# A cross-attention and MLP kernel: first MLP layer contracted over softmax slots, softmax with tokens on partitions, layers of different batches interleaved

## Chip, cores, metric

The kernel runs on one core of a Trainium2 chip. The metric is the device time of one execution in microseconds (us), lower is better. Each comparison uses executions of the kernel before on the same chip.

## The reference

Eight batches, eight heads, 512 tokens of 64 elements, and 32 state slots per head. Tokens attend to state slots, slots attend to tokens, the two results are stacked to 544 rows per batch with the heads side by side (512 wide), and an MLP with a leaky ReLU follows.

```python
B, H, S, Ns, D = (8, 8, 512, 32, 64)
scores = scale * x @ state.T                 # [B,H,512,32]
a = softmax(scores);  xread = a @ state      # token rows
a2 = softmax(scores.T over tokens); sread = a2 @ x   # state rows
x = concat([xread, sread], axis=2) -> [8*544, 512]
h = x @ w_in                                 # 512 -> 2048
g = maximum(0.01 * h, h)
out = g @ w_out                              # 2048 -> 512, float32
```

(Condensed; the reference subtracts the row maximum in each softmax, neither kernel does.)

## The kernel before

Attention is done for pairs of heads with the slots on partitions. Its result, `xbT`, is the MLP input, transposed. The MLP works on chunks of 512 rows, and its tiles are taken from a queue, one between any two attention pieces.

```python
# attention of a pair of heads (cut)
nc.tensor.matmul(sc[:], lhsT=BDT[:], rhs=xT[:])            # [64 slots, 512 tokens]
nc.scalar.activation(out=ET[:], in_=sc[:], func=Exp, scale=SCALE, accum_out=r2[:])
...  # r1c: sums over slots by matmul; pa: transpose of a2; psr: state rows
nc.tensor.matmul(xr[:], lhsT=st.BDbf[:], rhs=ET[:])        # unnormalised xread
...
nc.tensor.matmul(rr1b[:, t * P:(t + 1) * P], lhsT=bcl[:, t], rhs=ident[:])   # 1/sum, spread out
nc.vector.tensor_tensor(out=xbT[st.k][:, ...], in0=st.xr_sb[:], in1=rr1b[:], op=mult)

# first layer, one of 16 tiles of a chunk: K = 512, four matmuls (cut)
for kt in range(4):
    nc.tensor.matmul(ph[:, :n], lhsT=w_in_bf[kt][:, 128 * j:128 * (j + 1)],
                     rhs=xbT[kt][:, tok0:tok0 + n], start=(kt == 0), stop=(kt == 3))
nc.scalar.activation(out=t01[:, :n], in_=ph[:, :n], func=Identity, scale=0.01)
nc.vector.tensor_tensor(out=hT[:, j, :n], in0=ph[:, :n], in1=t01[:, :n], op=max)

# second layer, one of 4 tiles of a chunk
for j in range(16):
    nc.tensor.matmul(py[:], lhsT=hT[:, j, t * P:(t + 1) * P], rhs=w_out_bf[j][:], ...)
nc.scalar.copy(ysb[:], py[:]);  nc.sync.dma_start(out[r0:r0 + P, :], ysb[:])
```

The softmax here doesn't subtract the row's maximum and nothing guards it: scores larger than these inputs give would overflow.

## Time and profile before

| | before |
|---|---|
| median of the first runs | 348.24 us |
| span of the profiled run | 347.2 us |
| TensorE (PE) busy | 307.3 us, 88% |
| matmuls of the first layer | 512 of N=512, 64 of N=256 (as long as 544 of N=512) |
| matmuls of the second layer | 544 of N=512 |
| one middle batch | 35.25 us |

From the page of the kernel before: the line of busy times, the row of PE over 40 slices of the span (tenths of busy time, 9 is 90% or more), and the chain that ended last, by engine and by line (the view cuts this line short).

```profile
PE 307.3 (88%) x1821; PEld 142.0 (41%) x1856; DVE 188.9 (54%) x487; ACT 152.1 (44%) x371; POOL 29.5 (8%) x70
...
PE   0115678999999999999999999999999999999995
...
PE 84%; DMA 9%; issue 3%; DVE 2%; ACT 1%; ACTq 0%; DVEq 0%
PE ph L196 35%; PE py L217 33%; DMA w_out_stage<-in_moe_w_out_dram 4%; DMA w_in_stage<-in_moe_w_in_dram 4%; PE rr1b L175 3%; PE sc L106 3%; PE xr L137 2%; PE pa L143 2%; PE pxt L96 2%; PE r1c L129 2%; DMA stf<-in_state_dram 1%; PE psr L152 
```

From the eighth slice on PE is busy for 90% or more of nearly every slice, and it owns 84% of the chain. "Busy" counts the latency of pipelined matmuls, so the distance between starts is the better measure. From the timeline of PE (start, duration, what):

```profile
125.96 0.38 PE L196 MATMUL ph<-xbT_90,w_in_bf_94 128*128 128x512 bf16 x1
126.27 0.40 PE L106 MATMUL sc<-xT,BDT 128*64 128x512 bf16 x1
126.60 0.39 PE L196 MATMUL ph<-xbT_91,w_in_bf_95 128*128 128x512 bf16 x1
```

A 128x512 matmul is shown as 0.38 us long, but in an undisturbed row the next one starts 0.216 us later. Around the score matmul (the middle line), which uses 64 columns of the array, the starts are 0.31 and 0.33 us apart. Two lines of the chain in order of time, the same instruction in two successive batches, give the time of a batch:

```profile
180.05 0.34 PE rr1b L175 x4
...
215.30 0.34 PE rr1b L175 x4
```

Of its 35.25 us, 124 matmuls of 0.216 us are the MLP (26.8 us: 15 first-layer and 4 second-layer tiles, by the weight loads from 180.05 to 215.30), and 8.5 us are the attention, with small waits. A batch's share of the MLP is 136 matmuls; the loop takes only 19 tiles per batch from the queue, and the rest runs after the last attention. Busy time by stretch (length, then each engine, clock, DMA share, GB/s):

```profile
core 0: us, PE busy (x) PEld busy (x) DVE busy (x) ACT busy (x) POOL busy (x), PEclk, DMA share, GB/s
0.00:20.00 20.00, 1.33 (x6) 0.57 (x6) 6.89 (x16) 0.00 (x0) 6.42 (x14) 1.00 0.85 275
20.00:40.00 20.00, 10.00 (x61) 4.79 (x63) 11.06 (x36) 6.10 (x17) 1.85 (x5) 1.00 0.80 204
40.00:60.00 20.00, 15.59 (x96) 6.75 (x97) 13.47 (x39) 9.03 (x26) 2.60 (x6) 1.00 0.45 122
180.00:215.25 35.25, 34.62 (x214) 15.68 (x217) 20.39 (x56) 17.16 (x44) 3.24 (x8) 1.00 0.23 63
```

In the first 60 us PE is busy for 26.9; in the middle nearly always.

### The profile page before, as it was taken

The numbers are of one execution on the slowest core, as the hardware profiler recorded it, in microseconds if no ns is written. First come the engines' busy times: TensorE is split into PE (matmuls) and PEld (weight loads), VectorE is DVE, ScalarE is ACT, GpSimd is POOL, SyncE is SP. The second block draws the span as 40 slices with busy tenths as digits, with TensorE's granted clock in tenths as the row PEclk, the third lists the DMA queues.
The fourth block names the chain that finished last, engine by engine and source line by source line (L and its number), as shares of the span: only waits on it lengthen the run. The fifth ranks groups of instructions, "written<-read, shape, count | busy, mean of one in ns | idle before, by whom it ended". The sixth has DMA issues, their size and how long they took to land.

```text
span 347.2 us, 5237 instructions
## 1 busy us (share of the span) xinstructions
PE 307.3 (88%) x1821; PEld 142.0 (41%) x1856; DVE 188.9 (54%) x487; ACT 152.1 (44%) x371; POOL 29.5 (8%) x70
## 2 busy tenths in 40 slices
PE   0115678999999999999999999999999999999995
PEld 0012233444444444444444444444444444444472
DVE  0655468851795359724991289318951693084070
ACT  0032227632764256524653466326641662264171
POOL 0510111100100011000100010001000000000000
PEclk9999999999999999999999999999999999999999
DMA  7897563123222222213121312110001000100201
GB/s 274 250 261 208 131 188 74 32 67 93 65 61 55 74 64 49 47 64 91 41 58 64 93 33 61 35 69 23 1 33 60 32 0 30 71 21 16 77 31 60
DMA packets 44666, 26.55 MB, mean 76 GB/s; under 512 B 37728, under 2 KB 37728, under 8 KB 44128
## 3 DMA queue, kind: packets, MB, share of 16 engines
q1 hardware_dynamic: 41760, 17.84, 18.6%
q10 hardware_dynamic: 2880, 8.39, 7.2%
q8 instruction: 14, 0.23, 0.3%
q14 instruction: 12, 0.10, 0.1%
HBM read 17.30 MB, written 8.91 MB: 75 GB/s over the span
## 4 chain that ended last, share of the span: by engine, by line
PE 84%; DMA 9%; issue 3%; DVE 2%; ACT 1%; ACTq 0%; DVEq 0%
PE ph L196 35%; PE py L217 33%; DMA w_out_stage<-in_moe_w_out_dram 4%; DMA w_in_stage<-in_moe_w_in_dram 4%; PE rr1b L175 3%; PE sc L106 3%; PE xr L137 2%; PE pa L143 2%; PE pxt L96 2%; PE r1c L129 2%; DMA stf<-in_state_dram 1%; PE psr L152 1%; PE pbd L101 1%; ACTq L64 0%; ACT ET L110 0%
## 5 line engine op out<-in xcount | busy, mean ns | idle before, releaser
L217 PEld LDWEIGHTS <-hT 128*128 128x128 bf16 x544 | 50.4, 98 | 59.6 <-issue 3.7
L224 ACT COPY ysb<-py 128x512 f32<-128x512 f32 x34 | 19.9, 585 | 86.7 <-PE py L217 60.4
L196 PE MATMUL ph<-xbT_90,w_in_bf_94 128*128 128x512 bf16 (+1 forms) x141 | 52.2, 372 | 1.0 <-DVE xbT_90 L181 0.8
L196 PE MATMUL ph<-xbT_89,w_in_bf_93 128*128 128x512 bf16 (+1 forms) x140 | 52.0, 374 | 1.0 <-DVE xbT_89 L181 0.4
L196 PE MATMUL ph<-xbT_91,w_in_bf_95 128*128 128x512 bf16 (+1 forms) x139 | 51.5, 373 | 0.3 <-DVE xbT_91 L181 0.2
L196 PE MATMUL ph<-xbT_88,w_in_bf_92 128*128 128x512 bf16 (+1 forms) x135 | 50.0, 374 | 0.4 <-issue 0.3
L110 ACT ACTIVATE ET<-sc 64x512 bf16<-64x512 f32 x32 | 18.9, 589 | 23.2 <-PE sc L106 20.1
L92 POOL CAST X2b<-X2f 128x512 bf16<-128x512 f32 x32 | 21.3, 664 | 75.6 <-PE psr L152 64.0
L98 DVE COPY xT<-pxt 128x512 bf16<-128x512 bf16 x32 | 13.3, 417 | 22.0 <-PE pxt L96 21.9
L196 PEld LDWEIGHTS <-w_in_bf_95 128*128 128x128 bf16 x144 | 14.1, 98 | 17.5 <-issue 6.7
L86 POOL MEMSET BDbf<- 64x128 bf16 x32 | 7.7, 244 | 143.5 <-PE xr L137 126.0
L196 PEld LDWEIGHTS <-w_in_bf_94 128*128 128x128 bf16 x144 | 14.2, 99 | 13.6
L129 PE MATMUL r1c<-hi,ET 64*128 64x2 bf16 x128 | 8.0, 164 | 13.2 <-ACT ET L110 12.8
L139 ACT CAST xr_sb<-xr 128x512 bf16<-128x512 f32 x32 | 18.9, 590 | 1.5 <-PE xr L137 0.3
L87 DVE CAST BDbf<-stf 32x64 bf16<-32x64 f32 x32 | 6.1, 191 | 24.3 <-POOL BDbf L86 15.4
L101 PE MATMUL pbd<-ident,BDbf 64*128 64x64 bf16 x32 | 6.4, 201 | 13.0 <-DVE BDbf L88 10.7
L196 PEld LDWEIGHTS <-w_in_bf_92 128*128 128x128 bf16 x144 | 14.2, 99 | 8.0 <-issue 1.8
L196 PEld LDWEIGHTS <-w_in_bf_93 128*128 128x128 bf16 x144 | 14.1, 99 | 8.1 <-issue 1.0
L129 PEld LDWEIGHTS <-ET 64*128 64x128 bf16 x128 | 5.3, 95 | 28.6 <-ACT ET L110 25.7
L106 PE MATMUL sc<-xT,BDT 128*64 128x512 bf16 x32 | 13.8, 430 | 3.2 <-DVE xT L98 2.4
L165 DVE CAST bcl<-rr1c 128x512 bf16<-128x512 f32 x32 | 14.2, 444 | 0.8
L96 PE MATMUL pxt<-ident,X2b 128*128 128x128 bf16 x128 | 13.7, 233 | 0.0
(489 smaller groups left out, 568.1 us busy)
## 6 DMA issues: line engine op xcount, KB each, us to landing
out_dram<-ysb SPq DMA_DIRECT2D x34, 256.0 KB, 2.0
X2f<-in_x_dram SPq DMA_DIRECT2D x64, 128.0 KB, 2.7
w_in_stage<-in_moe_w_in_dram ACTq DMA_DIRECT2D x4, 1024.0 KB, 6.2
w_out_stage<-in_moe_w_out_dram ACTq DMA_DIRECT2D x16, 256.0 KB, 3.2
stf<-in_state_dram SPq DMA_DIRECT2D x64, 8.0 KB, 1.9
```

Of the source, the lines that this page charges most:

```text
L92: nc.gpsimd.tensor_copy(X2b[:], X2f[:])
L96: nc.tensor.transpose(pxt[:, t * P:(t + 1) * P], X2b[:, t, :], ident[:])
L98: nc.vector.tensor_copy(xT[:], pxt[:])
L106: nc.tensor.matmul(sc[:], lhsT=BDT[:], rhs=xT[:], start=True, stop=True)
L110: nc.scalar.activation(out=ET[:], in_=sc[:], func=mybir.ActivationFunctionType.Exp, scale=SCALE, accum_out=r2[:],)
L129: nc.tensor.matmul(r1c[:, 2 * t:2 * t + 2], lhsT=ET[:, t * P:(t + 1) * P], rhs=hi[:], start=True, stop=True,)
L139: nc.scalar.copy(xr_sb[:], xr[:])
L165: nc.vector.tensor_copy(bcl[:], rr1c[:, :].rearrange("p (t h) -> p t h", h=2)[:, :, :, None].to_broadcast([P, 4, 2, D]),)
L175: nc.tensor.matmul(rr1b[:, t * P:(t + 1) * P], lhsT=bcl[:, t, :, :].rearrange("p h d -> p (h d)"), rhs=ident[:], start=True, stop=True,)
L196: nc.tensor.matmul(ph[:, :n], lhsT=w_in_bf[kt][:, 128 * j:128 * (j + 1)], rhs=xbT[kt][:, tok0:tok0 + n], start=(kt == 0), stop=(kt == 3),)
L217: nc.tensor.matmul(py[:], lhsT=hT[:, j, t * P:(t + 1) * P], rhs=w_out_bf[j][:], start=(j == 0), stop=(j == 15),)
L224: nc.scalar.copy(ysb[:], py[:])
```

## The change

Because the token rows are `a @ state`, the first layer is `a @ (state @ w_in)`. The change computes M = state @ w_in per batch (256 slots x 2048) and contracts the normalised softmax `a` with it: K is 256 instead of 512, so two matmuls per tile. `a` is computed with tokens on partitions and transposed once. The state rows of all batches are gathered and go through the MLP together. The leaky ReLU is one ACT instruction. First-layer tiles of batch b+2 and attention of b+3 stand between second-layer quarters of b. Inputs are loaded in larger pieces.

```diff
+    def m_chunk(b, n):                     # M = state @ w_in, 64x32 array tiles
+        pm = psum.tile([P, 2, 512], FP32, name="pm", tag="big")
+        for k in range(NK):
+            for g in range(2):
+                sl = slice(64 * g, 64 * (g + 1))
+                nc.tensor.matmul(pm[32 * k:32 * (k + 1), g, :], lhsT=bd[sl, b, k, g, :],
+                                 rhs=w_in_bf[n][sl, k, :], start=True, stop=True)
+        nc.vector.tensor_copy(st.M[n][:], pm[:])
 ...
-                for kt in range(4):
-                    nc.tensor.matmul(ph[:, :n], lhsT=w_in_bf[kt][...], rhs=xbT[kt][...], ...)
-                nc.scalar.activation(out=t01, in_=ph, func=Identity, scale=0.01)
-                nc.vector.tensor_tensor(out=hT, in0=ph, in1=t01, op=max)
+        for g in range(2):
+            nc.tensor.matmul(ph[:], lhsT=st.M[n][:, g, P * jj:P * (jj + 1)], rhs=st.aT[:, g, :],
+                             start=(g == 0), stop=(g == 1))
+        nc.scalar.activation(out=st.hT[:, j, :], in_=ph[:], func=Prelu, alpha=0.01)
 ...
+    load_state(); load_x(0); load_w_in(0); load_x(1); load_w_in(1); load_x(2) ...   # casts on DVE
+    for b in range(AHEAD):                 # AHEAD = 2
+        cast_x(b); att_xT(b, 0); att_xT(b, 1); att_scores(b); att_sread(b); att_aT(b)
+    ...                                    # M and first layer of batches 0 and 1
+    for b in range(B):
+        for t in range(4):
+            for q in range(4):
+                ffn2(b, t, q)
+                if b + AHEAD < B:
+                    ffn1(b + AHEAD, 4 * t + q)
+                for f in pieces.get(4 * t + q, []):      # attention and M of batch b + 3
+                    f()
```

The order that the tile scheduler builds differs somewhat from this order at the start.

## The prediction

> **What bounds the kernel now.** TensorE. The page has PE busy 88% of a 347.2 us span, granted clock full in every slice, and the chain of waits is 84% PE (first layer 35%, second 33%). The timeline shows N=512 matmuls starting 216 ns apart. Each layer has 544 (the profile's weight loads of the second), so 1088 x 216 ns = 235 us. The rest is the attention's small matmuls and a bad start: by the stretches table PE is busy only 27 of the first 60 us while DMA moves about 200 GB/s in 256-byte packets. One middle batch takes 35.25 us (rr1b at 180.05, 215.30).
>
> **Removed.** Token rows: first layer contracts over K=256 (2 matmuls per tile instead of 4). 8x16x2=256 matmuls, 55.3 us, plus state rows 64 of N=256 (about 109 ns, half of 216), 7.0 us, against 117.5 us. xr, rr1b, pbd, pa, r1c and their evictions go. The leaky ReLU becomes one ACT instruction (585-590 ns, as the 128x512 evictions now take) instead of ACT and a 692 ns DVE max.
>
> **Added.** M = state @ w_in: 32 groups of 8 matmuls, 64 rows x 32 columns, N=512. Serial would be 8x216=1.73 us a group, 55 us in all. The built order keeps the 8 tiles of a group adjacent in the steady part, each at its own array position. The Trainium skill, "TensorE: Matmul & The Clock Gate", Part 3, gives measured packing gains (4 row tiles 3.07x, 16 tiles 10.6x); nothing in this trace shows it. "TensorEngine Tiling (Array Packing)", Key Properties, says that a change of tiling mode drains TensorE; the trace agrees: around the 64-column score matmul starts are 310-330 ns apart instead of 216. I take 0.6 us per group. Other attention per batch: 32 matmuls of N=128 at 60 ns (four transposes took 0.24 us) and 32 of N=64 at 28 ns (four sread matmuls took 0.11 us): 2.9 us.
>
> **Critical path.** Start: DVE runs in a fixed order in which weight casts stand between the softmax steps of batches 0 and 1, so these wait for DMA. At about 310 GB/s (estimate; the early stretches reach 330-362 at best) the third w_out part lands near 41 us, and only behind its cast come the softmax of batch 1 and the first M eviction. I expect dense FFN matmuls from about 46 us. Then 32 first-layer tiles without second-layer work are bound by ACT: 32 x 0.6 = 19 us, to about 65 us. Left for PE: second layer 544 x 216 ns = 117.5, first layer 6 x 6.9 = 41.5, state rows 7, attention 17.3, M 24 x 0.6 = 14.4: 198 us, plus 2 for stalls, 3 for the tail. 65+198+5 = 268 us. Batches in the middle should take 13.8+6.9+2.9+2.4 = 26 us instead of 35.25; ACT (about 10.5 us) and DVE (about 12.5) stay far below.
>
> **What would show it.** Second-layer starts 216 ns apart; M groups 0.4-0.8 us from first to following start; 25-27 us per middle batch; chain over 70% PE, with DMA/DVE owning the first 40-50 us; DVE under 130 us, ACT about 100 us with one table load.
>
> **What would make it wrong.** M tiles run one after the other: +1.1 us x 24 groups, about 295 us. Only pairs overlap: about 278. Start less blocked: 250-255. PSUM rotation stalling PE: 5-15 us more.
>
> Predicted 268 us, 80% range 250 to 290. Chances: faster by over 2% 0.97, within 2% 0.02, slower 0.01.

## The result

| | before | changed |
|---|---|---|
| median | 348.12 us | 270.49 us |
| range of 4 runs | 347.94 to 349.43 | 269.64 to 270.58 |
| span | 347.2 | 267.9 |
| a middle batch | 35.25 us | 25.23 us |

(The two middle batches do not hold the same share of the MLP: 124 matmuls of 136 before; after, all 96 of the token rows, while the state rows come later.) The ratio is 0.7762, 95% interval 0.7744 to 0.7781. Ratios here are the mean time of one kernel's fast runs over that of the other's of the same rounds, so not quite the ratio of the medians that are quoted. 268 had been predicted.

The same parts of the page of the changed kernel:

```profile
PE 229.3 (86%) x1640; PEld 113.6 (42%) x1640; DVE 123.8 (46%) x147; ACT 88.3 (33%) x153; POOL 19.5 (7%) x23
...
PE   0015264999999999999999999999999999999994
...
PE 79%; DVE 9%; DMA 8%; ACT 1%; issue 1%; DVEq 0%; ACTq 0%
PE py L240 40%; PE ph L216 21%; PE pm L199 4%; DMA w_stage<-in_moe_w_in_dram 4%; PE pxt L129 3%; PE phs L225 3%; PE pys L252 3%; DMA xf<-in_x_dram 2%; DMA w_stage<-in_moe_w_out_dram 2%; DVE A L153 2%; PE pat L186 2%; PE sc L141 1%; ACT E L1
```

The chain is still TensorE, at 79%. Its first-layer share fell from 35% to 21%; the second layer, unchanged in work, is now 40%. Three stretches (before the first first-layer matmul, the first dense stage, one middle batch), columns as before:

```profile
0.00:47.79 47.79, 13.65 (x153) 11.15 (x153) 24.60 (x34) 3.33 (x3) 10.94 (x15) 1.00 0.98 324
47.79:65.77 17.98, 17.90 (x96) 6.05 (x97) 7.23 (x6) 12.72 (x23) 0.00 (x0) 1.00 0.14 45
100.00:125.23 25.23, 25.23 (x193) 12.23 (x192) 13.83 (x16) 10.47 (x17) 2.24 (x2) 1.00 0.12 43
```

The middle batch is solid PE. From its timeline, a group of M between matmuls of the layers:

```profile
125.23 0.59 PE L216 MATMUL ph<-aT,M_952 128*128 128x512 bf16 x2
125.75 0.41 PE L199 MATMUL pm<-w_in_bf_92,bd 64*32 64x512 bf16 x8
126.10 1.04 PE L240 MATMUL py<-w_out_bf_93,hT 128*128 128x512 bf16 x4
```

The 8 matmuls of M start at 125.75 and the next matmul starts at 126.10: 0.34 us for 8. Before them, 90 ns are lost to the change of tiling (two first-layer matmuls from 125.23 would end their slots at 125.66). A group thus costs 0.43 us.

An account of the 79.3 us of span, worked out from starts and counts: first layer 544 x 0.216 = 117.5 before, 256 x 0.216 + 64 x 0.108 = 62.2 after, so 55.3 us. A middle batch's time beyond the two layers is 35.25 - 124 x 0.216 = 8.5 us before, and after it is 25.23 - 96 x 0.216 = 4.5 us, M included: 8 x 4.0 = 32 us. The two together are 8 us more than was gained, so the remainder (start, end and order) grew by about 8 us: the first first-layer matmul comes at 47.79 instead of 33.00. This is an account, not a proof; the experiments test its first term, M and the start. That the reworked attention gives 32 us was not tested by a run of its own.

The start of the changed kernel, from its chain in order of time (start, us, what):

```profile
6.65 10.95 DMA w_stage<-in_moe_w_in_dram
...
18.76 0.43 DVE stb L87
...
20.95 1.88 PE pxt L129 x16
...
25.24 5.60 DMA w_stage<-in_moe_w_out_dram
...
34.32 1.72 PE pxt L129 x16
...
40.69 1.13 DVE w_out_bf_95 L119
...
47.79 1.89 PE ph L216 x4
```

Reading down: wait for the second w_in part and its cast, the state cast behind it, the transposes and softmax of batch 0 with a wait for a w_out load inside (25.24), then the same steps for batch 1 (34.32 on, again with a weight cast inside, 40.69), and only then the first layer, at 47.79.

### The profile page after: what moved, and what is told of

Read it like the earlier page. It is cut to its first block, busy times and chain, and to the rows that moved or that the text cites. A ratio compares the mean times of both kernels' runs of the same rounds, so it can differ in the third digit from the quotient of the medians.

```text
span 267.9 us, 3811 instructions
## 1 busy us (share of the span) xinstructions
PE 229.3 (86%) x1640; PEld 113.6 (42%) x1640; DVE 123.8 (46%) x147; ACT 88.3 (33%) x153; POOL 19.5 (7%) x23
## 4 chain that ended last, share of the span: by engine, by line
PE 79%; DVE 9%; DMA 8%; ACT 1%; issue 1%; DVEq 0%; ACTq 0%
PE py L240 40%; PE ph L216 21%; PE pm L199 4%; DMA w_stage<-in_moe_w_in_dram 4%; PE pxt L129 3%; PE phs L225 3%; PE pys L252 3%; DMA xf<-in_x_dram 2%; DMA w_stage<-in_moe_w_out_dram 2%; DVE A L153 2%; PE pat L186 2%; PE sc L141 1%; ACT E L145 1%; DVE xT L134 1%; PE pr L168 1%; PE pr L162 1%
## 5 line engine op out<-in xcount | busy, mean ns | idle before, releaser
L207 ACT ACTIVATE hT<-ph 128x512 bf16<-128x512 f32 x128 | 75.0, 597 | 104.2 <-PE ph L216 104.2
L245 DVE COPY ysb<-py 128x512 f32<-128x512 f32 x32 | 22.1, 692 | 61.2 <-PE py L240 61.2
L240 PE MATMUL py<-w_out_bf_95,hT 128*128 128x512 bf16 x128 | 33.5, 381 | 0.0
L240 PE MATMUL py<-w_out_bf_94,hT 128*128 128x512 bf16 x128 | 33.2, 380 | 0.0
L240 PE MATMUL py<-w_out_bf_93,hT 128*128 128x512 bf16 x128 | 33.2, 380 | 0.0
L240 PE MATMUL py<-w_out_bf_96,hT 128*128 128x512 bf16 x128 | 32.9, 380 | 0.0
L107 POOL CAST xb<-xf 128x1024 bf16<-128x1024 f32 x16 | 17.0, 1092 | 118.7 <-issue 55.2
L145 ACT ACTIVATE E<-sc 128x1024 bf16<-128x1024 f32 x8 | 8.2, 1023 | 27.2 <-PE sc L141 27.2
L134 DVE COPY xT<-pxt 128x2048 bf16<-128x2048 bf16 x8 | 9.8, 1225 | 15.3 <-PE pxt L129 15.3
L129 PE MATMUL pxt<-ident,xb 128*128 128x128 bf16 x128 | 12.1, 242 | 0.7 <-DVE bd L92 0.7
L129 PEld LDWEIGHTS <-xb 128*128 128x128 bf16 x128 | 9.9, 110 | 4.7 <-issue 1.4
L141 PE MATMUL sc<-bd,xT 128*128 128x64 bf16 x128 | 5.8, 205 | 2.6 <-DVE xT L134 2.6
L162 PE MATMUL pr<-E,osel 128*128 128x128 bf16 x64 | 5.8, 241 | 2.3 <-ACT E L145 2.2
```

The source lines that it names most:

```text
L107: nc.gpsimd.tensor_copy(st.xb[:, :, 4 * hh:4 * hh + 4, :], src)
L129: nc.tensor.transpose(st.pxt[:, k, t, :], st.xb[:, t, 2 * k:2 * k + 2, :].rearrange("p h d -> p (h d)"), ident[:])
L134: nc.vector.tensor_copy(st.xT[:], st.pxt[:])
L141: nc.tensor.matmul(sc[:, t, :, k, :], lhsT=st.xT[:, k, t, :], rhs=bd[:, b, k, :, :], start=True, stop=True)
L145: nc.scalar.activation(out=st.E[:], in_=sc[:], func=ACTF.Exp, scale=SCALE)
L162: nc.tensor.matmul(pr[:, 1, 0, :], lhsT=osel[:, g, :], rhs=st.E[:, t, g, :, :].rearrange("p k n -> p (k n)"), start=(i == 0), stop=(i == 7))
```

## Experiments

Theory: TensorE is the limit before and after; the time fell because the first layer has half the matmuls and M is nearly free by packing. Rivals: the gain comes from elsewhere (eviction, interleaving, the start), or M costs much of the saving. For the start: DVE's fixed order with casts, against arrival of the data, against a chain of dependent steps. All ten kernels gave correct results. "Changed" below means 270.49. The diffs are cut and lines joined. The experiments ran in three later sessions on three chips, each with its own runs of the kernel before (medians 348.46 to 348.81); a difference from the changed kernel is therefore uncertain by up to about 1 us (e4: 3.1 us by the medians, 3.9 by the ratios; e9: 18.7 and 18.4).

### e1: the first layer's matmuls doubled

```diff
-        for g in range(2):
+        for i, g in enumerate((0, 1, 0, 1)):       # start at i == 0, stop at i == 3
             nc.tensor.matmul(ph[:], lhsT=st.M[n][:, g, ...], rhs=st.aT[:, g, :], ...)
-        lrelu(st.hT[:, j, :], ph[:])
+        lrelu(st.hT[:, j, :], ph[:], scale=0.5)
```

> The changed kernel with every first-layer tile of token rows accumulated twice (4 matmuls instead of 2, the activation scales by 0.5, so the result stays right). Theory, TensorE is the limit in the steady part: each middle batch takes 32 x 0.216 = 6.9 us longer (32.1 us instead of 25.23), and the whole kernel 48 to 55 us longer than 270.5, so about 321 us; the lower end if part of the start hides behind ACT. Rival, the first layer has slack behind ACT or DVE and the gain came from elsewhere: under 25 us longer.

320.74 us (one run), 50.3 us longer. The period of a middle batch, from the timeline of PE, the same transposes one batch apart:

```profile
119.26 0.61 PE L129 MATMUL pxt<-ident,xb 128*128 128x128 bf16 x8
...
151.40 0.61 PE L129 MATMUL pxt<-ident,xb 128*128 128x128 bf16 x8
```

That is 32.14 us, 6.9 more than 25.23, as 32 matmuls of 0.216 us should cost. First-layer matmuls are on the critical path one for one in the steady part. The rival falls. Over the whole kernel 128 tiles with two more matmuls each would make 55.3 us. Most of what is missing lies before 119.26, where the scheduler built another order (the second layer begins at 57.32 instead of 65.77), so the middle batch is the cleaner measure.

### e2: M without packing

```diff
-                nc.tensor.matmul(pm[32 * k:32 * (k + 1), g, :], lhsT=bd[sl, b, k, g, :],
-                    rhs=w_in_bf[n][sl, k, :], start=True, stop=True)
+                nc.tensor.matmul(pm[:, g, :], lhsT=bz[:, b, k, g, :],   # 128x128, zero-padded
+                    rhs=w_in_bf[n][:, k, :], start=(k == 0), stop=(k == NK - 1))
```

(`bz` is filled on POOL at the start; to make room, output buffers went from 3 to 2 and `rr2` from 2 to 1.)

> The changed kernel with M made by full-array matmuls: zero-padded 128x128 weights, 4 accumulating matmuls per half, so 8 of N=512 per group that cannot overlap, in the same places. Theory, the 8 tiles of a group run at once (0.34 us for 8 in the trace): a group takes 8 x 0.216 = 1.73 us, a middle batch 25.23 + 4 x 1.3 = 30.4 us, the kernel 33 to 42 us longer, about 308 us. Rival, packing is worth little (groups hidden behind other waits): under 12 us longer.

305.56 us (one run), 35.1 us longer. From the timeline of PE:

```profile
117.18 0.61 PE L135 MATMUL pxt<-ident,xb 128*128 128x128 bf16 x8
...
147.53 0.61 PE L135 MATMUL pxt<-ident,xb 128*128 128x128 bf16 x8
```

A batch takes 30.35 us, 5.1 more, or 1.28 for each of its four groups, as 1.73 us (eight unpacked matmuls of 0.216) instead of 0.43 should cost. Against the 0.34 us of the packed matmuls alone this is a factor of about 5, with the loss on the way in a factor of 4.0. Without packing nearly half the total gain would be lost.

### e3: the layers of different batches not interleaved

```diff
-        for t in range(4):
-            for q in range(4):
-                ffn2(b, t, q)
-                ffn1(b + AHEAD, 4 * t + q); pieces of attention
+        for i in range(16):
+            ffn1(b + AHEAD, i); pieces of attention
+        for t in range(4):
+            for q in range(4):
+                ffn2(b, t, q)
```

> The changed kernel with the program order of the main loop undone: for each batch first all 16 first-layer tiles of batch b+2 with the attention pieces of b+3, then all 16 second-layer quarters of b. Theory 1, interleaving hides ACT: a tile without second-layer work goes at about 0.64 us (ACT 0.6 and the handover, as at 61 to 65 us of the trace) instead of 0.43, so 16 x 0.21 = 3.3 us per batch, 18 to 20 us in all, about 290 us. Theory 2, the attention and M matmuls (4.6 us per batch), which stand between the tiles in the new order too, already fill that gap: under 6 us longer, within 2% of 270.5.

278.16 us (ratio to before 0.7965, 0.7945 to 0.7985): 7.7 us, or 2.8%, longer. This lies between the two theories. The built order did not undo all of the interleaving: in a middle batch 7 of the 64 second-layer matmuls still stand between first-layer tiles, so 7.7 us is the price of most of the interleaving, not of all of it. From the timeline of PE (in brackets: idle before, and who ended it), a middle batch and the stage after the last attention:

```profile
129.95 0.61 PE L129 MATMUL pxt<-ident,xb 128*128 128x128 bf16 x8
...
138.93 0.62 PE L186 MATMUL pat<-ident,A 128*128 128x128 bf16 x8 [0.87 <-DVE A L153]
...
156.51 0.61 PE L129 MATMUL pxt<-ident,xb 128*128 128x128 bf16 x8
...
216.58 0.59 PE L216 MATMUL ph<-aT,M 128*128 128x512 bf16 x2
217.01 0.60 PE L225 MATMUL phs<-srT,w_in_bf 128*128 128x256 bf16 x4
...
217.86 0.59 PE L216 MATMUL ph<-aT,M 128*128 128x512 bf16 x2
```

The middle batch takes 26.56 us, 1.33 more; 0.87 of it is one wait, of the transposes of `A` for the softmax on DVE. With less work between its own steps the latency of the attention shows. The rest of the 1.33 us (0.46) is not accounted for. Three batches show this wait (at 91.02, 112.36 and 138.93), the two after them do not. About half of the 8.7 us by which the span grew is lost after the last batch's transposes (182.26, against 177.86 in the changed kernel), most of it in the stage of the last three lines. There a tile of token rows and one of state rows take 1.28 us (216.58 to 217.86), where their matmuls and one of the second layer need 1.08; ACT is busy for 0.98 of it (0.60 and 0.38), and one tile is marked as waiting for ACT. So there theory 1 holds: the handover between TensorE and ACT shows where little else fills the gap. Interleaving hid both, the latency of the attention and this handover, and was worth about 10% of the gain.

### e4: weight casts on POOL

```diff
-        nc.vector.tensor_copy(w_in_bf[n][:], st[:])     # and w_out_bf
+        nc.gpsimd.tensor_copy(w_in_bf[n][:], st[:])     # cast_x(0), cast_x(1) right after their loads
```

> The changed kernel with the eight weight casts moved from DVE to POOL, which then makes all input casts in order of arrival; the order on TensorE stays the same. Theory 1, the start is blocked by DVE's fixed order, casts that wait for DMA standing before the softmax of batches 0 and 1: the first first-layer matmul comes at 26 to 34 us instead of 47.8, and the kernel gets 8 to 18 us faster than 270.5 (253 to 262). Theory 2, the start is bound by the 13.5 MB of input at about 340 GB/s, so w_out lands at 44 to 48 us anyway: the first-layer tiles move forward but the second layer does not, under 4 us gained.

267.35 us (0.765, 0.7623 to 0.7676): 3.1 us gained. Theory 1 falls: with no weight cast left on DVE, the first first-layer matmul came at 44.92 us, not at 26 to 34. Theory 2 got the size right, but said that the first-layer tiles would move far forward, which they did not. The chain of this kernel shows what held them:

```profile
10.06 7.66 DMA stf<-in_state_dram
...
21.71 1.88 PE pxt L129 x16
...
32.24 1.72 PE pxt L129 x16
...
44.92 1.48 PE ph L216 x3
```

The state landed only at 17.7 us, and from there two attention chains run one after the other (transposes at 21.71 and 32.24, 10.5 us apart; the second takes 12.7 us up to the first layer), nearly every step waiting for the one before.

### e5: the single-instruction leaky ReLU alone, on the kernel before

```diff
-                nc.scalar.activation(out=t01, in_=ph, func=Identity, scale=0.01)
-                nc.vector.tensor_tensor(out=hT, in0=ph, in1=t01, op=max)
+                nc.scalar.activation(out=hT, in_=ph, func=Prelu, alpha=0.01)
```

> The kernel before with one part of the change alone: the leaky ReLU as one ACT instruction instead of an ACT scaling and a DVE max. Theory, TensorE bounds the kernel before and this part only takes work off DVE: DVE busy falls from 189 us to about 95, ACT stays near 150, the time moves by less than 2% (345 to 350 us). Rival, the two-engine eviction held TensorE up through the PSUM buffers or DVE's queue delayed the attention: 8 to 20 us faster.

347.14 us (0.9964, 0.9936 to 0.9992): 0.4%. The busy times of its page:

```profile
PE 308.7 (89%) x1856; PEld 140.9 (41%) x1856; DVE 103.0 (30%) x343; ACT 151.8 (44%) x371; POOL 28.3 (8%) x70
```

DVE fell from 188.9 to 103.0 us, and the time hardly moved: work taken off an engine that nothing waits for. The rival falls.

### e6: the state loaded first

```diff
-                nc.scalar.dma_start(stf[...], state[...])
+                (nc.scalar if g else nc.sync).dma_start(stf[...], state[...])   # four on each queue, ahead of x
```

> The changed kernel with the eight state loads first on two queues, ahead of x and the weights, and nothing else (the scheduler then also puts the batch-0 softmax ahead of most weight casts on DVE). Theory, the start is a chain: state landed near 18 us, then two attention chains of 10 us one after the other: state lands by 9 us, the first first-layer matmul moves from 47.8 to 36 to 41 us and the kernel gains 6 to 11 us (260 to 264). Rival, the weights' arrival (the last w_out part at 46 to 50 us) bounds the start: under 3 us gained.

259.10 us (0.743, 0.740 to 0.746): 11.4 us gained, by the order of loads and what followed from it. The first first-layer matmul came at 35.72. The time from the issue of a state load to its landing, in the changed kernel and then here:

```profile
DMA to landing us min/median/max: 4.5/7.9/9.1
```

```profile
DMA to landing us min/median/max: 2.4/3.3/3.6
```

Half a megabyte in 256-byte pieces, issued through one queue beside the large loads, had its last load issued at about 10 us; in front of them, at 2.2. In this run the scheduler also placed the first softmax ahead of most casts, so the gain is of both; e4 shows that moving the casts alone gives 3 to 4 us when the state is late. What they give when it is early was not separated.

### e7: as e6, attention of batches 0 and 1 side by side

```diff
     for b in range(AHEAD):
         cast_x(b); att_xT(b, 0); att_xT(b, 1)
-        att_scores(b); att_sread(b); att_aT(b)
+    for b in range(AHEAD): att_scores(b)
+    for b in range(AHEAD): att_sread(b)
+    for b in range(AHEAD): att_aT(b)
```

> As the state-first kernel, and the attention steps of batches 0 and 1 stand side by side instead of one batch after the other. Theory of the chain: the second 10 us chain mostly disappears, the first first-layer matmul comes at 28 to 34 us, the kernel gains a further 5 to 8 us (253 to 258). Rival, the weights bound it: within 2 us of the state-first kernel.

256.72 us (0.7365, 0.7342 to 0.7389): 2.4 us, less than half of what was expected; a miss, although the first first-layer matmul came at 33.98, just within the range. The chain:

```profile
4.47 10.28 DMA xf<-in_x_dram
...
20.31 2.27 DVE r L147 x2
...
24.64 1.14 DVE w_in_bf L113
...
33.98 1.89 PE ph L216 x4
```

Both batches now wait for x of batch 1, which lands at 14.75 us, and then for DVE, on which the reductions (20.31), multiplies and reciprocals of two batches, with weight casts (24.64, 27.77), follow each other almost without a gap. The chain of latencies became a queue on one engine.

### e8: as e7, with the casts on POOL

The edit is that of e4 on top of e7.

> As the paired kernel, and all weight casts on POOL. Theory of the chain: DVE no longer waits for DMA between softmax steps, the first first-layer matmul at 24 to 30 us, the kernel at 249 to 255. Rival: with attention early, the second layer waits for the last w_out part, cast by the slower POOL at about 50 us, so no gain over the paired kernel, or a loss of 1 to 3 us.

255.24 us (0.7341, 0.7302 to 0.7379), not told apart from e7 by the intervals. In the profiled execution the first first-layer matmul came at 35.26, not at the 24 to 30 us expected, and later than in e7. But this execution was the slowest of the four (257.68 us; the others 255.0 to 255.3), so it may overstate the start. From the timeline of DVE and POOL:

```profile
24.66 4.61 DVE L153 TENSOR_TENSOR A<-E,rr 128x1024 bf16<-128x1024 bf16 x2
25.31 5.71 POOL L113 CAST w_in_bf<-w_stage 128x2048 bf16<-128x2048 f32 x2
```

Two multiplies for `A` took 4.61 us, where one takes 1.22 us when POOL is idle; POOL was casting all the time. The Trainium skill, "Advanced Engine Details and Errata", GPSIMD Details, says that POOL shares a read and a write interface with DVE and conflicts with DVE instructions that have two SBUF inputs. This multiply has two (`E` and `rr`), and the trace agrees. It also shows that the order decides. In the changed kernel six of the eight multiplies took 1.22 us; two of these were still running when a cast of x began, and it was the cast that took longer (1.26 and 1.28 us instead of 1.04). The two multiplies that began during a cast took 1.97 and 1.98, and each ended 1.08 us after that cast (cast 42.67 to 43.70, multiply 42.81 to 44.78). Here, too, the second multiply ends 1.08 us after the cast during which it began (28.19 and 29.27). So the later one appears to wait for the other to end, though spans on POOL are rough in these profiles.

### e9: as e6, batch 0 goes on without waiting for batch 1

```diff
-    # attention 0, attention 1, then M and first layer of 0 and 1 by column block
+    for f in attn_pieces(0).values(): f()
+    for b in range(AHEAD):
+        for n in range(4):
+            m_chunk(b, n)
+            for j in range(4 * n, 4 * n + 4):
+                ffn1(b, j); attention piece of b + 1, if one is due at j
```

> As the state-first kernel (259.1), and first-layer work of batch 0 starts as soon as its own attention is done, with the attention of batch 1 between its tiles, then batch 1 with the attention of batch 2. Theory, the wait for batch 1 is the rest of the start's loss: the first first-layer matmul comes at 22 to 25 us instead of 35.7 and the kernel takes 246 to 252 us. Rival, the weights now bind: the built order puts second-layer matmuls ahead of batch 1's first layer, they wait on TensorE for the last w_out part at 45 to 48 us, and the kernel takes 254 to 260.

251.75 us (0.7234, 0.7196 to 0.7273), 7.4 us below e6 and 18.7 below the changed kernel: the best version here. PE:

```profile
24.02 1.45 PE L216 MATMUL ph<-aT,M 128*128 128x512 bf16 x4
...
34.47 0.85 PE L240 MATMUL py<-w_out_bf,hT 128*128 128x512 bf16 x3 [2.66 <-DVE w_out_bf L119]
```

The first first-layer matmul comes at 24.02, and the built order did put second-layer matmuls early, as the rival said, but they waited 2.66 us for the first w_out cast and no more.

### e10: as e9, three staging buffers for weights

```diff
-        st = stage.tile(..., name="w_stage", tag="w_stage", bufs=2)
+        st = stage.tile(..., name="w_stage", tag="w_stage", bufs=3)     # and xf with bufs=2
```

> As the batch-0-first kernel, with three staging buffers for weights and two for x instead of two and three, so that the weights land ahead of the x of batches 3 and 4. If the weights' arrival binds, the last w_out part lands 5 to 8 us earlier (39 to 42 us) and the kernel is 4 to 8 us faster than the batch-0-first kernel; if not, within 1.5 us of it.

251.98 us (0.7242, 0.7204 to 0.7280). The last w_out cast started at 42.9 instead of 45.3 us, less of a move than expected, and the time is that of e9. So 2.3 us of earlier weights gain nothing here; whether the buffer taken from x cost something was not separated.

## Why the prediction was right

- **Limit: TensorE, before and after.** Right. e5 shows that DVE's work before was free, e1 that first-layer matmuls are paid for one by one.
- **First layer halved.** Right in size: 117.5 us before against 62.2; putting two matmuls per tile back cost 50.3 us, and in a middle batch the 6.9 us that the count gives.
- **M at 0.6 us a group.** The packing works; 0.43 us was measured, against 1.73 unpacked (e2: 35.1 us over the whole kernel).
- **Attention 2.9 us and batch 26 us.** 25.23 us was measured. Without 20.74 us of layers and 1.72 us of M groups, 2.8 us are left for attention, where 8.5 us went to it before.
- **Dense first-layer matmuls from about 46 us, because of casts on DVE.** The time was right (47.8), the cause only in small part. e4 took the casts away and gained 3 to 4 us. The late state and two dependent attention chains in a row were the larger part, as far as the runs separate them: e6 and e9 moved the first matmul to 35.7 and 24.0.
- **Then ACT-bound for 19 us, to about 65.** The second layer did start at 65.8, but after 24 tiles, not 32, and ACT was busy only 12.7 of 18 us. The timeline of PE in that stage:

```profile
52.78 0.39 PE L199 MATMUL pm<-w_in_bf_90,bd 64*32 64x512 bf16 x2
53.10 0.60 PE L216 MATMUL ph<-aT,M_367 128*128 128x512 bf16 x2
...
62.24 0.59 PE L216 MATMUL ph<-aT,M_449 128*128 128x512 bf16 x2
...
63.52 0.59 PE L216 MATMUL ph<-aT,M_476 128*128 128x512 bf16 x2
```

  Until 61 us single M matmuls stand between pairs of first-layer matmuls, and one or two of them take 0.32 us of PE (52.78 to 53.10), nearly the price of a whole group of 8. From 62 us two tiles take 1.28 us (62.24 to 63.52), 0.64 each; ACT is busy for 1.09 us of it and waits for PE in the rest. So this stage was slowed by broken-up M groups first and by the handover to ACT later. Both causes were read from starts; no run removed the fragments alone (in e1 they are gone, but there the first layer is doubled).
- **198 us left after the start.** The last matmul's slot ends near 264.0 us, 198 after 65.8. This agreed by compensation: eight first-layer tiles more were left (3.5 us), and M cost 26 x 0.43 = 11.2 us instead of 14.4. That the sum of 268 came so near is thus partly luck: the start ended on time for another reason than the one given, and these two errors cancelled.
- **DVE under 130, ACT about 100, chain over 70% PE.** 123.8, 88.3 and 79%: ACT was overestimated.

The forecast did not price interleaving by itself; e3, which undid most of it, puts it at 7.7 us.

## What to carry to other kernels

When one operand of a chain of products is itself a product with a small inner dimension, reassociate to contract over it, and check that the extra product can be packed into array tiles: here packing decided 35 of 78 us, and only while the tiles of a group stay adjacent. When TensorE is the limit, count its matmul starts; work taken from engines that nothing waits for brings almost nothing (e5). Count also how much of the work a "middle batch" holds before comparing two of them: 124 matmuls of 136 here. Read the start of a kernel as a chain of its own: the small load that everything needs goes first, and the first batch should run on without waiting for the second (18.7 us together).

## What the Trainium skill lacked or had wrong

- "TensorE: Matmul & The Clock Gate", Part 3, The mechanism: it says that weight loads overlap with matmuls in flight only when the row group differs. Here the 8 tiles of a group (two row groups, four column groups each) took 0.34 us from the first start to the next matmul; waiting within a row group would be four times 0.216, 0.86 us. The eight weight loads are recorded within 0.11 us, the matmuls of the same row groups being in flight. (The paragraph above this statement does allow for a background weight buffer.) It also has no figure for 64x32 tiles: about 5x against unpacked here, 4.0x with the loss on the way in.
- "TensorEngine Tiling (Array Packing)", Key Properties: a change of tiling mode drains TensorE, without a price. Here about 90 ns at the way into a group, and one or two tiled matmuls alone between full ones cost 0.32 us.
- "TensorE: Matmul & The Clock Gate", Back-to-back issue gap: gives about 131 ns for a sustained N=512 matmul beside the isolated 216 ns, and about 81 ns for N=128. The isolated figure is the one that fits: the undisturbed streams here run at 216 ns, and eight transposes of N=128 took 0.45 us (from 127.40 to 127.85 in the changed kernel), 56 ns each.
- "Advanced Engine Details and Errata", GPSIMD Details: this section gives the conflict of POOL with DVE no size and does not say who waits (who waits is told elsewhere in the skill, so that lack is of this section alone). Here a 1.22 us multiply of two SBUF inputs took 1.97 us when it began during a cast of x and 1.22 us when the cast began after it, and two took 4.61 us beside casts that did not stop.
- No figure was found for the time that small loads take to land beside large ones: the state loads took 7.9 us (median) to land beside the large loads and 3.3 us ahead of them.
